# Two attention layers on one core: fewer, wider matmuls in the sums and the probability transposes, 256-wide visits, and the fetch of instructions in the builder's clock

## The chip, the cores and the metric

The kernel runs on one core of one Trainium2 chip. The metric is device time in microseconds (us). Two runs of the kernel before took 3495.84 and 3511.78 us, median 3503.81 us. A separate execution was recorded by the hardware profiler; every row in this document is from it.

## What is computed

The input x has 2048 rows of 512. Four layers follow each other, A, B, A, B, each on a layer-normalised x and added to x:

```
# A: 64 segments of 32 rows, one after the other; mem (8 rows) is handed on
for s in range(64):
    h = concat([mem, xs[s]])              # 40 x 512
    q, k, v = h @ Wq, h @ Wk, h @ Wv      # 32 heads of 128
    p = softmax(mask(q @ k.T * scale))    # 40 x 40 per head
    o = (p @ v) @ Wo
    mem = o[:8];  out[s] = o[8:]
# B: plain attention over all 2048 rows, 32 heads of 16, no mask
p = softmax(q @ k.T * 0.25);  out = (p @ v) @ wo
```

A is a recurrence: segment s+1 needs `mem` of segment s. B has no order of its own: a pair of a query block and a key block can be done as soon as both rows exist.

## The kernel before, in words

One Python program writes the instructions of all engines. For TensorE (PE) it fixes the order by hand: a planner (`step`, line 372) keeps a clock for PE, ScalarE (ACT) and VectorE (DVE), `Clock` (line 40), with a cost in us for every group of instructions, and emits whichever group its clock says is ready.

**A segment of A** is cut into groups that `segment` (line 698) takes from a list, PLAN or PLAN_PAIRS (lines 638 and 639). Q0 to Q3 and K0 to K3 (`qk_group`, line 525) project eight heads each: 32 matmuls of 128x128 weights with 40 columns, into one PSUM bank, which ACT or DVE then copies to `a_QT` or `a_KT`. S0 and S1 (`s_group`, line 562) make the scores of 16 heads each; ACT takes the exponential, and DVE masks, sums and scales it into `a_pn`. T0 and T1 (`pt_group`, line 589) transpose the probabilities with matmuls against the identity. V0 and V1 (line 552) project the values, P0 and P1 (or the pairs A and B; lines 608 and 619) multiply probabilities and values, and W0 to W3 (line 630) apply Wo. After W3, DVE writes the next segment's memory rows (line 743). A segment has 608 matmuls, each preceded by its weight load: 1216 rows on PE.

A matmul that needs only part of the 128x128 array is placed in a part of it by `tile_position`: in S and T of the kernel before, four matmuls stand side by side in column tiles of 32. The query of a head has 40 rows, so S needs two of these tiles for each head.

**Layer B in the gaps.** When a tile of 128 rows has come out of A, `tile_done` (line 867) projects it to B's q, k and v, stores them in device memory, and `visits` (line 839) adds the pairs of blocks that have become possible as runs; c is the group of 512 rows that the tile belongs to, r its place in it. A run is one query block (128 to 512 wide) of eight head pairs against a list of key tiles, cut into units of at most 512 columns. A unit (`emit_qk`, line 424) is 4 matmuls for each key tile, an exponential on ACT in two instructions (lines 437 and 440), and 4 matmuls of probabilities with values (`pv_mm`, line 443), which add up in one PSUM bank, `b_oacc`. At a run's end DVE adds `b_oacc` to what was stored of that block. `quota` (line 689) says how many units a segment should take in, at most 13. With five units or more the segment uses PLAN_PAIRS.

The second A starts when the first B has finished its first 512 rows, and the second B's last units run alone after the last segment.

## Time and profile before

| | us |
|---|---|
| median of two runs | 3503.81 |
| the two runs | 3495.84, 3511.78 |
| profiled execution, its own time | 3476.14 |
| its span, first to last instruction | 3474.4 |
| PE busy (matmuls) | 3066.5 |
| ACT busy | 2491.6 |
| DVE busy | 1555.3 |

The profiled execution was 27.7 us shorter than the median of the two runs. "PEld" is the loading of weights, which overlaps the matmuls. In a row of a group, "x" is the number of instructions, then come the busy time, the mean duration of one in ns, and the idle time of the engine just before them with what ended it. "issue" there means that the engine waited for nothing that the profile shows. The duration of a matmul includes its way through the array; matmuls follow each other more closely than that.

### The profile page before, as it was taken

The page shows a single profiled execution, that of the slowest core. Times are in us where ns is not written, and L with a number is a line of the kernel's source. Part 1 is how long each engine was busy: PE and PEld are TensorE (multiplying, and loading weights), DVE is VectorE, ACT ScalarE, POOL GpSimd, SP SyncE. Part 2 cuts the span into 40 slices and gives each one's busy share as a digit, 9 for nine tenths or more (in the row PEclk, how much of TensorE's full clock was granted, in tenths as well). Part 3 has the DMA queues.
Part 4 walks back from the last instruction along what each step waited for, and adds up shares of the span by engine and source line. Part 5 has one row for each costly group of instructions (what it writes and reads, how often), then busy time and mean ns, then how long its engine had stood idle before and what let it go on. Part 6 is the DMA issues. An engine that isn't in the chain of part 4 may idle for free. (4 is left out here: it accounts for less than half of the span.)

```text
span 3474.4 us, 218836 instructions
## 1 busy us (share of the span) xinstructions
PE 3066.5 (88%) x101019; PEld 2354.8 (68%) x101019; DVE 1555.3 (45%) x4220; ACT 2491.6 (72%) x3384; POOL 400.5 (12%) x677
## 2 busy tenths in 40 slices
PE   3888999899999889988889999989988899888998
PEld 2777777777676666656666767776666666666566
DVE  1223333355555445455445453435445455553411
ACT  1444667677778778867787676658777788887897
POOL 1000011111111111100111011111011111110000
PEclk9999999999999999989999999999999999999999
DMA  6000112232434335444343122324243343445431
GB/s 232 24 24 25 53 54 86 73 111 84 123 106 140 97 101 161 122 122 130 110 115 110 44 84 64 103 65 132 79 120 113 113 142 99 141 140 148 122 86 44
DMA packets 321695, 350.77 MB, mean 101 GB/s; under 512 B 95360, under 2 KB 248192, under 8 KB 320768
## 3 DMA queue, kind: packets, MB, share of 16 engines
q1 hardware_dynamic: 279792, 225.23, 23.2%
q0 software_dynamic: 35200, 102.55, 9.0%
q8 instruction: 791, 12.96, 1.6%
q10 hardware_dynamic: 5776, 8.91, 0.8%
q14 instruction: 136, 1.11, 0.1%
HBM read 234.02 MB, written 102.50 MB: 97 GB/s over the span
## 5 line engine op out<-in xcount | busy, mean ns | idle before, releaser
L437 ACT ACTIVATE b_pt<-b_SX 128x1536 bf16<-128x1536 f32 (+2 forms) x1040 | 1492.1, 1435 | 441.1 <-PE bank L435 401.5
L440 ACT ACTIVATE b_pt<-bank 128x512 bf16<-128x512 f32 (+2 forms) x1040 | 614.2, 591 | 1.4 <-PE bank L435 1.4
L533 PE MATMUL bank<-a_hT,a_Wq 128*128 128x40 bf16 x16384 | 504.1, 180 | 51.3 <-issue 20.7
L634 PE MATMUL bank<-a_OT,a_Wo 128*128 128x40 bf16 x16384 | 507.0, 183 | 47.8 <-ACT a_OT L249 24.1
L634 PEld LDWEIGHTS <-a_Wo 128*128 128x128 bf16 x16384 | 469.6, 98 | 97.4 <-issue 75.7
L533 PE MATMUL bank<-a_hT,a_Wk 128*128 128x40 bf16 x16384 | 504.4, 180 | 30.4 <-issue 21.6
L533 PEld LDWEIGHTS <-a_Wq 128*128 128x128 bf16 x16384 | 456.8, 96 | 102.0 <-issue 78.7
L533 PEld LDWEIGHTS <-a_Wk 128*128 128x128 bf16 x16384 | 456.5, 96 | 65.7 <-issue 54.8
L435 PE MATMUL b_SX<-b_q,b_k 32*128 32x128 bf16 (+2 forms) x6672 | 426.7, 271 | 46.2 <-ACT b_pt L437 18.1
L449 PE MATMUL b_oacc<-b_pt,b_v 128*17 128x128 bf16 (+2 forms) x8896 | 405.5, 272 | 28.4 <-issue 14.5
L435 PE MATMUL bank<-b_q,b_k 32*128 32x128 bf16 (+2 forms) x2224 | 414.9, 271 | 10.1 <-DVE a_KT L251 3.7
L251 DVE CAST a_OT<-bank 128x160 bf16<-128x160 f32 x689 | 194.8, 319 | 237.7 <-PE bank L604 231.7
L575 DVE TENSOR_TENSOR a_pn<-a_pn,c_mask 128x256 bf16<-128x256 bf16 x256 | 74.9, 293 | 498.0 <-ACT a_pn L573 497.6
L435 PEld LDWEIGHTS <-b_k 32*128 32x128 bf16 x8896 | 187.3, 94 | 160.2 <-issue 93.1
L548 PE MATMUL bank<-a_Wv,a_hT 128*32 128x512 bf16 x4096 | 272.6, 382 | 13.0 <-issue 7.9
L449 PEld LDWEIGHTS <-b_v 128*17 128x17 bf16 x8896 | 149.2, 90 | 175.7 <-issue 125.1
L813 DVE TENSOR_TENSOR b_ain<-b_oacc,b_ain 128x512 f32<-128x512 f32 (+2 forms) x248 | 165.5, 667 | 149.0 <-PE b_oacc L449 141.7
L818 POOL DMA_DIRECT2D b_A<-b_aout x200 | 108.7, 544 | 1066.7 <-DVE b_aout L806 902.2
L251 DVE CAST a_QT<-bank 128x320 bf16<-128x320 f32 x294 | 144.2, 490 | 187.1 <-PE bank L533 177.2
L818 POOL DMA_DIRECT2D b_A<-b_ain x176 | 95.7, 544 | 841.9 <-DVE b_ain L813 633.0
L251 DVE CAST a_KT<-bank 128x320 bf16<-128x320 f32 x259 | 126.8, 490 | 106.4 <-PE bank L533 89.8
L249 ACT CAST a_KT<-bank 128x320 bf16<-128x320 f32 x253 | 108.7, 430 | 91.2 <-PE bank L533 90.3
(111 smaller groups left out, 3484.9 us busy)
## 6 DMA issues: line engine op xcount, KB each, us to landing
b_ain<-b_A SPq DMA_DIRECT2D x224, 256.0 KB
b_A<-b_ain POOLq DMA_DIRECT2D x176, 256.0 KB, 3.1
b_k<-b_K SPq DMA_DIRECT2D x298, 128.0 KB
b_v<-b_V SPq DMA_DIRECT2D x456, 68.0 KB
b_q<-b_Q SPq DMA_DIRECT2D x240, 128.0 KB
b_A<-b_aout POOLq DMA_DIRECT2D x184, 64.0 KB, 2.6
a_rest<-a_vx POOLq DMA_DIRECT2D x64, 128.0 KB, 3.1
a_VR<-a_rest SPq DMA_DIRECT2D x512, 16.0 KB
```

The source lines that it names most:

```text
L249: self.nc.scalar.copy(dst, src)
L251: self.nc.vector.tensor_copy(dst, src)
L435: nc.tensor.matmul(out[t][:, j * qw:(j + 1) * qw], lhsT=k[32 * t:32 * t + 32, kj * 128:(kj + 1) * 128], rhs=q[32 * t:32 * t + 32, 0:qw], s ...
L437: nc.scalar.activation(pt[:, 0:NX, 0:w], self.SX[:, 0:NX, 0:w], ACT.Exp, scale=B_SCALE)
L440: nc.scalar.activation(pt[:, NX + i, 0:w], b.t[:, 0:w], ACT.Exp, scale=B_SCALE)
L449: self.nc.tensor.matmul(self.oacc[32 * t:32 * t + 17, 0:qw], lhsT=u.v[:, kj, 17 * t:17 * t + 17], rhs=u.p[:, t, j * qw:(j + 1) * qw], star ...
L533: nc.tensor.matmul(ps[:, u, :], lhsT=W[:, ft, h * DH:(h + 1) * DH], rhs=h_s[:, ft, 0:L], start=(n == 0) if ft_major else (ft == 0), stop=( ...
L548: self.nc.tensor.matmul(b.t[32 * t:32 * t + 32, :], lhsT=lhsT(ft), rhs=self.Wv[:, ft, n * 512:(n + 1) * 512], start=(ft == 0), stop=(ft == ...
L575: nc.vector.tensor_tensor(self.pn[:, st, :, M:L], self.pn[:, st, :, M:L], self.mask[:], ALU.mult)
L634: self.nc.tensor.matmul(ps[:, ft, :], lhsT=self.Wo[:, h, 128 * ft:128 * ft + 128], rhs=self.OT[:, h, :], start=(h == 0 and ft == 0), stop= ...
L813: nc.vector.tensor_tensor(acc[:, w], k.oacc[:, w], acc[:, w], ALU.add)
L818: nc.gpsimd.dma_start(B.Acc_d[self.qc][self.hg][:, self.qo:self.qo + self.qw], acc[:, w])
```

## The change

It has five parts.

1. **T**: one matmul transposes two heads. The identity's columns 0 to 39 and 64 to 103 are given as one operand of 80 columns (`sel`), so a T group has 16 matmuls of 80 columns where it had 32 of 40.
2. **S**: two column tiles of 64 in the place of four of 32, one matmul for each head: 16 matmuls where there were 32. `a_QT` gets 24 columns of padding behind every eight heads (`[128, 4, 8 * L + 24]`), because a tile of 64 reads 24 columns past the 40 of its head.
3. **B visits**: a query block of c > 0 that was taken as four runs of 128 columns is taken as two of 256, at r = 1 and r = 3. In the last group of 512 rows (c = 3) only r = 1 is 256 wide, and r = 2 and 3 stay at 128.
4. **The planner's clock** counts PE's instructions. At the 192nd of every 256 it notes the time, and the next 256 may not start before 3.7 us (`FETCH`) after that or after the fetch before. Each call of `pe` passes its number of matmuls, and some costs are changed by 0.02 to 0.1 us.
5. **The lists** PLAN and PLAN_PAIRS are in another order.

```
+FETCH = 3.7
 ...
     def pe(self, cost, ready, mode, n):
         t = max(self.t["PE"], ready) + (0.11 if mode != self.mode else 0.0)
         self.mode = mode
-        self.t["PE"] = t + cost
-        return t + cost + 0.18
+        left, per = 2 * n, cost / (2 * n)
+        while left:
+            step = min(left, (192 if self.count < 192 else 256) - self.count)
+            t, left, self.count = t + step * per, left - step, self.count + step
+            if self.count == 192:
+                self.ahead = t
+            elif self.count == 256:
+                t = max(t, self.fetched)
+                self.count, self.fetched = 0, max(self.fetched, self.ahead) + FETCH
+        self.t["PE"] = t
+        return t + 0.2
 ...
-        self.sel = [self.ident[:, 0:L], self.ident[:, 64:64 + L]]
+        self.sel = self.ident[:].rearrange("p (c r) -> p c r", c=2)[:, :, 0:L]
 ...
-        self.QT = bp.tile([128, H * L + 24], bf16, name="a_QT")
+        self.QT = bp.tile([128, 4, 8 * L + 24], bf16, name="a_QT")
 ...
+    def s_mm(self, ps, st, hp, ct):
+        h = 2 * (8 * st + hp) + ct
+        o = L * (h % 8)
+        self.nc.tensor.matmul(ps[64 * ct:64 * ct + 64, hp, :], lhsT=self.QT[:, h // 8, o:o + 64], rhs=self.KT[:, h, :], start=True, stop=True, tile_position=(0, 64 * ct))
 ...
         for hp in range(8):
-            for t in range(4):
-                h = 2 * (8 * st + hp) + t // 2
-                o = L * h + 32 * (t % 2)
-                nc.tensor.matmul(ps[32 * t:32 * t + 32, hp, :], lhsT=self.QT[:, o:o + 32], rhs=self.KT[:, h, :], start=True, stop=True, tile_position=(0, 32 * t))
-        done = ck.pe(0.29, max(at, self.s_at(st)), "PV")
+            for ct in range(2):
+                self.s_mm(ps, st, hp, ct)
+        done = ck.pe(0.27, max(at, self.s_at(st)), "col64", 16)
 ...
         for part in range(2):
-            for h4 in range(4):
+            for j in range(2):
                 for t in range(4):
-                    self.nc.tensor.matmul(ps[32 * t:32 * t + 32, 4 * part + h4, :], lhsT=self.pn[:, st, 2 * t + h4 // 2, 32 * part:32 * part + 32], rhs=self.sel[h4 % 2],
+                    self.nc.tensor.matmul(ps[32 * t:32 * t + 32, 4 * part + 2 * j:4 * part + 2 * j + 2, :], lhsT=self.pn[:, st, 2 * t + j, 32 * part:32 * part + 32], rhs=self.sel,
                                           start=True, stop=True, tile_position=(0, 32 * t))
 ...
-    PLAN = "Q0 K0 Q1 K1 S0 Q2 K2 Q3 K3 S1 T0 V0 P0 V1 T1 W0 P1 W1 W2 W3".split()
-    PLAN_PAIRS = "Q0 K0 Q1 K1 S0 Q2 K2 Q3 K3 S1 T0 V0 A0 B0 V1 T1 W0 A1 B1 W1 W2 W3".split()
+    PLAN = "K0 K1 Q0 Q1 Q2 S0 K2 Q3 K3 V0 S1 T1 T0 V1 P0 W0 P1 W1 W2 W3".split()
+    PLAN_PAIRS = "Q0 K1 K0 Q1 S0 Q3 K2 K3 Q2 S1 V1 T0 V0 B0 A0 T1 W0 A1 B1 W1 W2 W3".split()
 ...
-        if c > 0:
+        if c > 0 and (r == 1 or r == 3 and c < 3):
+            add(c, 128 * r - 128, 256, list(range(4 * c)))
+        elif c == 3 and r > 1:
             add(c, 128 * r, 128, list(range(4 * c)))
```

The planner then emits another order. Three places of it follow; what stands before and after is taken from the two built programs.

On PE, the start of the first T group of the program (`a_pn` holds the probabilities, `c_ident` is the identity). Before:

```order
L595 LDWEIGHTS a_pn
L595 MATMUL bank_222<-c_ident,a_pn 32x40
L595 LDWEIGHTS a_pn
L595 MATMUL bank_222<-c_ident,a_pn 32x40
L595 LDWEIGHTS a_pn
L595 MATMUL bank_222<-c_ident,a_pn 32x40
```

And of the change:

```order
L610 LDWEIGHTS a_pn
L610 MATMUL bank_220<-c_ident,a_pn 32x80
L610 LDWEIGHTS a_pn
L610 MATMUL bank_220<-c_ident,a_pn 32x80
L610 LDWEIGHTS a_pn
L610 MATMUL bank_220<-c_ident,a_pn 32x80
```

Each matmul writes 80 columns in the place of 40, and the group has 16 of them in the place of 32, each still with its own weight load.

On PE, the start of the first unit of the program whose query block is narrower than 512 (`b_SX` and a bank take the scores of the four row tiles). Before:

```order
L435 LDWEIGHTS b_k
L435 MATMUL b_SX<-b_q,b_k 128x128
L435 LDWEIGHTS b_k
L435 MATMUL b_SX<-b_q,b_k 128x128
L435 LDWEIGHTS b_k
L435 MATMUL b_SX<-b_q,b_k 128x128
L435 LDWEIGHTS b_k
L435 MATMUL bank_219<-b_q,b_k 128x128
```

And of the change:

```order
L447 LDWEIGHTS b_k
L447 MATMUL b_SX<-b_q,b_k 128x256
L447 LDWEIGHTS b_k
L447 MATMUL b_SX<-b_q,b_k 128x256
L447 LDWEIGHTS b_k
L447 MATMUL b_SX<-b_q,b_k 128x256
L447 LDWEIGHTS b_k
L447 MATMUL bank_222<-b_q,b_k 128x256
```

Such a unit has 8 score matmuls in the place of 16, and as many less with the values; its width on ACT, 512 columns, is the same.

On ACT, the third segment, which has no unit in it (`a_QT`, `a_KT`, `a_V` and `a_PT` are copies out of PSUM, the ACTIVATE is the exponential of S0 and of S1). Before:

```order
L249 CAST a_QT<-bank_220 128x320
L249 CAST a_KT<-bank_219 128x320
L249 CAST a_QT<-bank_222 128x320
L249 CAST a_KT<-bank_221 128x320
L249 CAST a_QT<-bank_220 128x320
L573 ACTIVATE a_pn<-bank_219 128x8x40
L249 CAST a_KT<-bank_222 128x320
L249 CAST a_QT<-bank_221 128x320
L249 CAST a_KT<-bank_220 128x320
L249 CAST a_PT<-bank_219 128x320
L249 CAST a_V<-bank_222 128x512
L573 ACTIVATE a_pn<-bank_221 128x8x40
```

And of the change:

```order
L261 CAST a_KT<-bank_219 128x320
L261 CAST a_KT<-bank_220 128x320
L261 CAST a_QT<-bank_222 128x320
L261 CAST a_QT<-bank_221 128x320
L261 CAST a_QT<-bank_219 128x320
L588 ACTIVATE a_pn<-bank_220 128x8x40
L261 CAST a_KT<-bank_222 128x320
L261 CAST a_QT<-bank_221 128x320
L261 CAST a_KT<-bank_219 128x320
L261 CAST a_V<-bank_220 128x512
L588 ACTIVATE a_pn<-bank_222 128x8x40
L261 CAST a_PT<-bank_221 128x320
```

The projections of K come first, the third Q group still stands ahead of S0, V0 comes ahead of S1, and T0 (`a_PT`) behind it.

Counted over both programs, PE's rows of the four layers, each matmul with its weight load (the kernel before has 2330 matmuls that only keep PE busy, the change 2509):

| rows on PE | before | change |
|---|---|---|
| S, 256 groups | 16384 | 8192 |
| T, 256 groups | 16384 | 8192 |
| units of B: scores and values | 35584 | 26368 |
| matmuls that keep PE busy | 4660 | 5018 |

And by stretch of the A layers, cut at the last Wo matmul of a segment (segments are counted from 0 over both A layers; units in equivalents of 512 columns):

| segments | rows before | rows of the change | units before | units of the change |
|---|---|---|---|---|
| 1 to 16 | 20096 | 18048 | 0 | 0 |
| 17 to 32 | 21376 | 18928 | 57 | 52 |
| 33 to 63 | 47296 | 40504 | 270 | 266 |
| 64 to 66 | 5832 | 5252 | 56 | 55 |
| 67 to 80 | 24284 | 21228 | 127 | 135 |
| 81 to 127 | 70972 | 60600 | 371 | 363 |
| behind the last | | | 143 | 153 |

Segments 53 to 55 have 5536 rows and 29 units before, and 4192 rows and 29 units in the change.

## Rows read from the trace of the kernel before

**Rows 1.** The page: span and busy time of each engine.

```profile
span 3474.4 us, 218836 instructions
PE 3066.5 (88%) x101019; PEld 2354.8 (68%) x101019; DVE 1555.3 (45%) x4220; ACT 2491.6 (72%) x3384; POOL 400.5 (12%) x677
```

**Rows 2.** The page: the chain that ended last, by engine.

```profile
PE 27%; issue 9%; ACT 9%; DVE 2%; DMA 1%; POOL 1%; SPq 0%; ACTq 0%; POOLq 0%; DVEq 0%
```

**Rows 3.** The page, DMA queues: packets, MB, share of 16 engines; PE's instructions.

```profile
q8 instruction: 791, 12.96, 1.6%
```

**Rows 4.** The same queue in the window 157 to 185 us.

```profile
q8 instruction: 8, 0.13, 1.8%
```

**Rows 5.** The same queue in the window 1081 to 1129 us.

```profile
q8 instruction: 12, 0.20, 1.8%
```

**Rows 6.** Timeline, PEld, 184 to 201 us: start, length, what, [idle before].

```profile
186.70 0.87 PEld L533 LDWEIGHTS <-a_Wq 128*128 128x128 bf16 x32
187.60 0.27 PEld L570 LDWEIGHTS <-a_QT 128*32 128x32 bf16 x31
...
195.06 0.85 PEld L634 LDWEIGHTS <-a_Wo 128*128 128x128 bf16 x31 [0.73 <-issue]
195.94 0.27 PEld L595 LDWEIGHTS <-a_pn 128*32 128x32 bf16 x32
196.25 0.87 PEld L634 LDWEIGHTS <-a_Wo 128*128 128x128 bf16 x32
197.15 0.10 PEld L604 LDWEIGHTS <-a_V 32*128 32x128 bf16 x4
...
197.32 0.10 PEld L604 LDWEIGHTS <-a_VR 8*128 8x128 bf16 x4
197.46 0.10 PEld L634 LDWEIGHTS <-a_Wo 128*128 128x128 bf16 x1
198.22 1.85 PEld L634 LDWEIGHTS <-a_Wo 128*128 128x128 bf16 x63 [0.66 <-issue]
```

**Rows 7.** Waits: engine and line, total us, times, longest us.

```profile
PEld L533 <- issue: 133.5, 320, 12.7
PEld L449 <- issue: 125.1, 429, 2.5
```

**Rows 8.** Busy time by stretch; window, length, PE PEld DVE ACT POOL, PEclk, DMA.

```profile
78.00:367.00 289.00, 252.72 (x10044) 217.54 (x10041) 89.62 (x260) 126.96 (x308) 21.69 (x32) 1.00 0.10 27
367.00:684.00 317.00, 291.42 (x10697) 234.86 (x10694) 122.05 (x336) 210.20 (x373) 34.13 (x55) 0.99 0.22 63
684.00:1451.00 767.00, 697.50 (x23658) 531.53 (x23655) 408.33 (x1081) 591.46 (x731) 106.31 (x183) 0.96 0.39 114
1451.00:1614.00 163.00, 138.72 (x2972) 90.55 (x2969) 85.28 (x248) 118.99 (x150) 15.18 (x26) 0.92 0.46 137
1614.00:1994.00 380.00, 337.27 (x12170) 264.11 (x12167) 186.91 (x515) 285.34 (x358) 40.47 (x67) 0.96 0.35 97
1994.00:3144.00 1150.00, 1032.05 (x35480) 790.87 (x35477) 567.87 (x1503) 867.92 (x1142) 151.81 (x259) 0.96 0.37 107
3144.00:3475.00 331.00, 293.15 (x5362) 207.49 (x5358) 83.49 (x240) 280.15 (x304) 19.87 (x35) 0.98 0.35 100
```

**Rows 9.** The same for segments 50 and 51, and 53 to 55.

```profile
1081.00:1129.00 48.00, 43.89 (x1392) 31.49 (x1390) 28.29 (x73) 43.07 (x51) 5.46 (x11) 1.00 0.56 166
1164.00:1246.00 82.00, 69.40 (x2779) 55.96 (x2772) 36.70 (x107) 60.72 (x70) 8.10 (x16) 0.96 0.28 76
```

**Rows 10.** Groups of instructions over the whole span.

```profile
L437 ACT ACTIVATE b_pt<-b_SX 128x1536 bf16<-128x1536 f32 (+2 forms) x1040 | 1492.1, 1435 | 441.1 <-PE bank L435 401.5 <-PE b_SX L435 14.4 <-PE bank L604 1.1
L440 ACT ACTIVATE b_pt<-bank 128x512 bf16<-128x512 f32 (+2 forms) x1040 | 614.2, 591 | 1.4 <-PE bank L435 1.4
L570 PEld LDWEIGHTS <-a_QT 128*32 128x32 bf16 x8192 | 99.6, 94 | 67.5 <-issue 23.6 <-ACT a_QT L249 11.6 <-DVE a_QT L251 9.7
```

More of the change, by code (lines that the diff above doesn't have):

```diff
@@ L45, in __init__, with pe @@
         self.mode = None
-    def pe(self, cost, ready, mode):
+        self.count, self.fetched, self.ahead = 0, 0.0, 0.0
+    def pe(self, cost, ready, mode, n):
         t = max(self.t["PE"], ready) + (0.11 if mode != self.mode else 0.0)
         self.mode = mode
-        self.t["PE"] = t + cost
-        return t + cost + 0.18
+        left, per = 2 * n, cost / (2 * n)
[9 more added lines that the diff above has]
+        return t + 0.2
     def cost(self, eng, n):
@@ L299, in transposes @@
             self.nc.tensor.transpose(ps[:, ft, :], xn[:, ft * 128:(ft + 1) * 128], self.ident[:])
-        done = self.ck.pe(0.25, max(ready, at), "full")
+        done = self.ck.pe(0.25, max(ready, at), "full", 4)
         dst(ps)
@@ L421, in keep_warm @@
             self.nc.tensor.matmul(b.t[:, 0:128], lhsT=self.ident[:], rhs=self.ident[:], start=True, stop=True)
-        b.free = ck.pe(0.056 * n, at, "full")
+        b.free = ck.pe(0.056 * n, at, "full", n)
     def emit_qk(self, u):
@@ L430, in emit_qk @@
         ys = [self.take() for _ in range(4 - NX)]
-        done = ck.pe(0.25, max([self.x_free, u.at, u.run.at] + [at for _, at in ys]), "S")
+        done = ck.pe(0.23, max([self.x_free, u.at, u.run.at] + [at for _, at in ys]), "S", 4 * len(u.kjs))
         out = [self.SX[:, i, :] for i in range(NX)] + [b.t[:] for b, _ in ys]
@@ L445, in pv_mm @@
         nj = len(u.kjs)
-        done = self.ck.pe(0.23, max(u.pt_at, self.o_free if u.first else 0.0), "PV")
+        done = self.ck.pe(0.23, max(u.pt_at, self.o_free if u.first else 0.0), "PV", 4 * nj)
         for j, kj in enumerate(u.kjs):
@@ L623, in pv_pair @@
         dst = self.pv_mms(st, ts, [b.t[:] for b, _ in bs])
-        done = self.ck.pe(0.26, max([ready] + [at for _, at in bs]), "S")
+        done = self.ck.pe(0.19, max([ready] + [at for _, at in bs]), "S", 16)
         w = 4 * L
@@ L665, in a_ready @@
         return max(t, self.bank_at())
-    MODE = {"Q": "full", "K": "full", "W": "full", "S": "PV", "T": "PV", "V": "PV", "P": "S", "A": "S", "B": "S"}
+    MODE = {"Q": "full", "K": "full", "W": "full", "S": "col64", "T": "PV", "V": "PV", "P": "S", "A": "S", "B": "S"}
     def a_pick(self, left):
@@ L878, in xo @@
                 nc.tensor.transpose(ps[:, ft, :], k.oTa[:, ft, :], k.ident[:])
-            done = ck.pe(0.25, max(at, k.at["oTa"]), "full")
+            done = ck.pe(0.25, max(at, k.at["oTa"]), "full", 4)
             xr = k.lnp.tile([128, 512], A.dt, name="a_xr", tag="xin", bufs=2)
@@ L898, in proj @@
                     nc.tensor.matmul(ps[:, g, :], lhsT=k.WB[:, ft, col + 128 * g:col + 128 * g + 128], rhs=k.hB[:, ft, :], start=(ft == 0), stop=(ft == 3))
-            return b, ps, ck.pe(0.95, at, "full")
+            return b, ps, ck.pe(0.95, at, "full", 16)
         c, r = divmod(Tt, 4)
@@ L919, in vv @@
                 nc.tensor.matmul(b.t[:], lhsT=k.hB[:, ft, :], rhs=k.WB[:, ft, 1024:1536], start=(ft == 0), stop=(ft == 3))
-            done = ck.pe(0.87, at, "full") + 0.2
+            done = ck.pe(0.87, at, "full", 4) + 0.2
             b.free = k.evac(k.vst[:, :, :, 0:16], b.t[:].rearrange("p (a b d) -> p b a d", b=2, d=16), 512, done, "DVE")
@@ L945, in tq @@
                 nc.tensor.transpose(ps[:, q, :], acc[:, 128 * q:128 * q + 128], k.identf[:])
-            done = ck.pe(0.09 * nq, at, "full")
+            done = ck.pe(0.11 * nq, at, "full", nq)
             v = ps[:, 0:nq].rearrange("p q (t s) -> p q t s", s=32)
@@ L982, in a @@
                 nc.tensor.transpose(ps[:, f, :], k.Osb[:, qs, f * 128:(f + 1) * 128], k.ident[:])
-            done = ck.pe(0.25, max(at, ready), "full")
+            done = ck.pe(0.25, max(at, ready), "full", 4)
             st["o"] = k.lnp.tile([128, 4, 128], bf16, name="b_OT", tag="t", bufs=3)
@@ L991, in b @@
                 nc.tensor.matmul(b.t[:], lhsT=st["o"][:, f, :], rhs=k.WoB[:, f, :], start=(f == 0), stop=(f == 3))
-            done = ck.pe(0.87, at, "full") + 0.2
+            done = ck.pe(0.87, at, "full", 4) + 0.2
             x = k.accp.tile([128, 512], self.out_dt, name="b_xo", tag="acc")
@@ L1024, in softmax @@
             for ct in range(2):
-                h = 2 * (8 * st + hp) + ct
-                nc.tensor.matmul(ps[64 * ct:64 * ct + 64, hp, :], lhsT=k.QT[:, L * h:L * h + 64], rhs=k.KT[:, h, :], start=True, stop=True, tile_position=(0, 64 * ct))
+                k.s_mm(ps, st, hp, ct)
         t = k.lnp.tile([128, 8, L], f32, name="g_t")
```

12 lines of the change are left out of this document (6 added, 6 removed).

## The prediction

> **What bounds the kernel now.** The page's busy shares come first [rows 1]: PE is busy for 88% of the span, ACT for 72%, and no other engine reaches half. A busy PE need not be at its limit, so the chain of waits comes next [rows 2]: PE 27% and ACT 9% of the span are on the chain with work, but 9%, some 310 us, is "issue", time in which PE waited for nothing that the profile shows. PE's instruction queue explains it [rows 3]: 791 packets of 12.96 MB are 16.4 KB each, and 791 x 256 = 202,496 is PE's number of rows (twice 101,019 by [rows 1]). So PE's program arrives in blocks of 256 rows. In a stretch without any unit of B, 8 blocks came in 28 us [rows 4]: 3.5 us a block, 13.7 ns a row. The timeline shows who waits [rows 6]: two "issue" gaps of 0.73 and 0.66 us at 195.06 and 198.22, and between them 31 + 32 + 32 + 32 (eight rows of four) + 1 = 128 loads, with their matmuls 256 rows, exactly a block. PE had finished one block and the next was not there. The largest sums of such waits are 133.5 and 125.1 us [rows 7]. At 3.5 us, 791 blocks are 2770 us, more than ACT's 2491.6.
>
> The limit is not the same everywhere. In segments 50 and 51, with 10 or 11 units each, 12 blocks came in 48 us [rows 5], 4.0 us a block, so the fetch had slack, and ACT was busy for 43.07 of 48 us [rows 9]: there ACT limits. In segments 53 to 55 with nearly as many units, but narrow ones, 5536 rows at 13.7 ns are 76 of 82 us and ACT is at 74% [rows 9]: there the fetch limits. The stretches [rows 8] give the mixture: ACT is busy for 44% in segments 1 to 16, 66% in 17 to 32, and 75 to 77% from 33 on (73% in 64 to 66, around the change of layers).
>
> **What the change removes.** By the tables of the order, S and T lose 8192 PE rows each, the units of B 9216, and 358 keep-warm rows are added: 25,242 fewer, 12%. No column less passes through PE: S had eight rounds of four matmuls of 40 columns and has eight rounds of two; T had eight rounds of 40 and has four of 80; a unit has half the matmuls, twice as wide. So what is saved is nearly all fetch, at 13.7 ns a row, and only where the fetch limits. By stretch, full value first, then the share that I take:
>
> - Segments 1 to 16: 2048 rows, 28 us. ACT is idle for more than half the time, so nearly all counts; the turn of the recurrence at each segment's end stays. 0.9: 25 us.
> - 17 to 32: 2448 rows, 33.5 us. ACT has room on the whole. 0.85: 28 us.
> - 33 to 63: 6792 rows, 93 us. The share is taken from segments 53 to 55: they lose 1344 rows, 18.4 us, so the fetch would allow 82 - 18 = 64 us; but their 29 units, at the 48 / 21 = 2.29 us a unit that segments 50 and 51 needed, want 66 us, and two limits so close do not overlap fully; I put them at 70, a saving of 12 of 18.4, or 0.65. Segments that ACT limits already give less; 0.6: 56 us.
> - 64 to 66: 580 rows, 8 us; the ends of the first B stand in it. 0.6: 5 us.
> - 67 to 80: 3056 rows, 42 us, but eight units more, each 1.435 + 0.591 = 2.03 us on ACT [rows 10]. 0.5: 21 us.
> - 81 to 127: 10,372 rows, 142 us, like 33 to 63. 0.6: 85 us.
>
> That is 220 us. **What it gives back:** 153 units in the place of 143 stand behind the last segment, where ACT is busy for 85% [rows 8]; ten at 2.03 us cost 20 us. The sum is 200 us less.
>
> **What I cost at nothing.** The padding of `a_QT`: S0 reads 24 columns that the third Q group writes, and its loads waited 11.6 + 9.7 us for those copies [rows 10]. The fetch goes on during such a wait, so these 21 us are mostly part of the fetch's time; between 0 and 21 us, I take 0. The wider tile of S: from the last projection load (its row of 32 loads ends at 187.57 with one of about 0.10 us, so it starts at 187.47) to the first load of S at 187.60 [rows 6] are 0.13 us, against 0.025 us between loads within a group: a change of tiling costs 0.10 us. S1 now stands with a tiling of its own among V and T, two changes more in each of 128 segments, 26 us of PE time. They fall where PE waits for blocks or for ACT; between 0 and 26 us, I take 0. "TensorEngine Tiling (Array Packing)" of the Trainium skill, under Key Properties, says that changing the tiling mode drains the engine, not just changing the tile. The gap in this row agrees; a sum that let every drain be felt would have 174 us for the gain. The fewer loads and stores of B and the fewer ends of runs on DVE: DMA is 1% of the chain and DVE 2% [rows 2], 0 us. The lists and the planner's clock move V0 ahead of S1 and T0 behind it, so that T0, V1, P0 and W0 lie beside S1's softmax; that and where units are placed could cost as well as gain. ACT's largest idle sum is 401.5 us of waits for the scores [rows 10]; I let a tenth of it, 40 us, go either way and take 0.
>
> **The number.** The profiled execution took 3476 us; less 200 is 3276. The median of the runs was 27.7 us higher than that execution, and the change should be measured like it: **3304 us**, 5.7% less. Unknown sizes: with every share at 1 the gain is 347 - 20 + 21 = 348 us, 3156 us; with 0.9 and 0.6 in the first two stretches, 0.3 from 33 on and 0 in 67 to 80, it is 25 + 20 + 28 + 2 + 43 - 20 = 98, less 26 for the tilings, 72 us, 3432 us. I expect neither end: the first needs ACT to limit nothing, the second sets segments 53 to 55 at half of what their rows allow. The forecast's own range is 3215 to 3425.
>
> **Rivals.**
>
> - *ACT takes over at once.* If every segment from 33 on behaves like 50 and 51, only the first 32 gain: 25 + 28 - 20 = 33 us, 3471 us. For it: ACT is at 90% there, and the number of units is the same. Against it: 53 to 55 have as many units and take 3.3 us a segment longer, with ACT at 74%. Chance 0.12.
> - *The blocks are not the limit.* If the gaps of PE come from elsewhere and a block always arrives in time, fewer rows save nothing and the ten late units cost 20 us: 3524 us. For it: the profile names no releaser of these gaps. Against it: 256 rows between two gaps and 3.5 us between blocks, whatever PE does in between. 0.07. The Trainium skill has this as its rule: "Runtime: NRT & Kernel Launch", Instruction fetch mechanics, says that the next block is fetched while the present one runs and that the cost of crossing a block is mostly hidden. By that rule the rival's time holds; the trace here disagrees, with 0.73 and 0.66 us lost at two crossings.
> - *The planner gains more.* With a clock that knows the fetch, ACT waits less for its scores: all shares near 0.9 and 40 of the 401.5 us are about 330 us, 3174 us. For it: the old clock knew no fetch and placed units by times that were too early. Against it: the order is only as good as its costs, and 3.7 us stands where the trace has 3.5. 0.08.
> - *Slower: the clock of PE.* PE's granted clock is 1.00 in segments 1 to 16, but 0.92 in 64 to 66, 1 being 2.4 GHz and a half 1.2 GHz [rows 8]. With the same work in fewer rows and ACT limiting more, PE may stand still more often and fall to the lower level; a microsecond there costs up to half a microsecond. To lose the 200 us and 70 more, PE needs 540 us more at 1.2 GHz, a mean clock about 0.08 lower than now: 3574 us. It decides from there. Against it: in segments 1 to 16 PE has no matmul running for 13% of the time, and the clock stays at 1.00. 0.04.
>
> **Chances.** The forecast has 0.69. A measurement of this kernel can tell about 2% from no change, that is 70 us: faster is below 3434. The range that holds 8 of 10 takes in the forecast, most of the planner's case and the part of ACT's case nearest to the forecast: 3185 to 3440. Faster: 0.69 + 0.08 + a quarter of ACT's case, 0.80. Same: the rest of it and the hidden fetch, 0.16. Slower: 0.04.
>
> **What would show it.** PE's instruction queue should have about (202,038 - 25,242) / 256 = 691 packets. In segments 1 to 16 the spacing of blocks should stay near 3.5 us, and a segment without units take 15.4 in the place of 17 us. In segments 53 to 55 ACT should rise to about 85% and the time fall to 70 us. The waits of S's loads for `a_QT` should be gone. The stretch behind the last segment should be some 20 us longer. I am wrong if the blocks become rarer and the segments are not shorter, if ACT's idle time before the scores grows by as much as the fetch gives, or if the granted clock falls below 0.9.

## The result and the profile after

The kernel after the change takes **3344.9 us** (median of two runs, 3343.7 and 3346.1) against 3503.8 before, a ratio of 0.955 with a 95% interval of 0.945 to 0.964. Predicted were 3304 us. In the sets of runs below, the kernel before was run 29 more times: medians of 3517.6, 3516.1 and 3516.8 us in three sets, single runs from 3501 to 3530. The changed kernel, run again beside them, took 3345.5, a ratio of 0.953 (0.949 to 0.957). So the change is worth about 171 us, of which 159 showed against the two runs of before that the prediction had.

**A caution about the rows of before.** The profiled execution of before (span 3474.4) is shorter than all of those 29 runs. A comparison by stretch with [rows 8] alone is therefore some 40 us too small in sum. One experiment (`p6_act_load`, below) runs the instructions of before unchanged from segment 17 on and gives a second profile of them; the table below uses both.

**The page.** Span, engines, and PE's instruction queue (packets, MB, share), to be set beside [rows 1] and [rows 3]:

```profile
span 3344.4 us, 192793 instructions
PE 3058.7 (91%) x88348; PEld 2263.6 (68%) x88398; DVE 1526.7 (46%) x4077; ACT 2495.4 (75%) x3439; POOL 357.7 (11%) x597
...
q8 instruction: 693, 11.35, 1.4%
```

98 blocks of 256 rows fewer, 693 in the place of 791; 691 were predicted. PE is busy for 3058.7 us, before for 3066.5: what went is almost all time in which PE stood idle (286 us of the span, 408 before).

Busy time by stretch, after, as in [rows 8]: window, length, PE PEld DVE ACT POOL, PEclk, DMA. The windows end at the last Wo matmul of segments 16, 32, 63, 66, 80 and 127:

```profile
78.00:350.50 272.50, 247.60 (x9020) 212.36 (x9023) 90.83 (x263) 122.70 (x304) 21.68 (x32) 0.99 0.11 28
350.00:653.00 303.00, 285.15 (x9478) 226.19 (x9479) 126.34 (x337) 195.60 (x356) 30.86 (x49) 0.98 0.21 61
653.00:1386.00 733.00, 693.14 (x20257) 502.19 (x20259) 387.25 (x1006) 595.39 (x763) 90.43 (x154) 0.95 0.37 108
1386.00:1545.00 159.00, 135.94 (x2644) 84.75 (x2648) 84.86 (x243) 113.61 (x144) 17.18 (x30) 0.90 0.48 138
1545.00:1915.00 370.00, 338.98 (x10638) 254.76 (x10641) 188.98 (x515) 298.89 (x374) 35.66 (x59) 0.96 0.34 94
1915.00:3005.00 1090.00, 1023.17 (x30297) 748.36 (x30308) 553.01 (x1435) 858.89 (x1155) 131.44 (x221) 0.95 0.35 102
3005.00:3345.00 340.00, 311.04 (x5449) 217.77 (x5453) 83.64 (x239) 299.74 (x324) 19.36 (x34) 0.99 0.35 96
```

Every stretch up to segment 127 is shorter, the one behind it is longer, and ACT's share rises where B is dense (33 to 63: from 77% to 81%). The column PEclk says that the granted clock did not rise: 0.95 and 0.95 in the two long stretches, against 0.96 and 0.96.

In us, each stretch by the two profiles of either kernel (before: the profile shown ahead and `p6_act_load`; after: its profile and that of `after_again`), and the last column for `u4_old_lists`, the changed kernel with before's lists of group order:

| segments | before | after | gain, of the means | predicted | gain of `u4_old_lists` |
|---|---|---|---|---|---|
| 1 to 16 | 289.3 | 272.9, 270.7 | 17.5 | 25 | 18.1 |
| 17 to 32 | 316.9, 326.7 | 302.7, 300.6 | 20.1 | 28 | 19.2 |
| 33 to 63 | 767.0, 771.9 | 732.6, 733.5 | 36.4 | 56 | 49.9 |
| 64 to 66 | 162.6, 162.6 | 159.6, 161.1 | 2.3 | 5 | 2.8 |
| 67 to 80 | 379.8, 389.6 | 370.1, 369.2 | 15.0 | 21 | 16.0 |
| 81 to 127 | 1150.6, 1158.3 | 1090.0, 1092.0 | 63.5 | 85 | 78.8 |
| behind 127 | 330.0, 329.3 | 338.9, 339.5 | -9.6 | -20 | -27.6 |

The sum of the gains is 145 us; some 26 of the 171 of the medians lie in the difference between these two profiles of before and its usual run. For segments 1 to 16 there is a second profile of before's instructions too, `p3_visits_256` below, which has the same ones there and took 301.4 us at a granted clock of 0.95 (289.3 at 1.00). The gain of 17.5 us is the one at a like clock.

Groups of the page after, which answer to the first two of [rows 10] (busy, mean ns | idle before, releaser):

```profile
L449 ACT ACTIVATE b_pt<-b_SX 128x1536 bf16<-128x1536 f32 (+1 forms) x1040 | 1493.7, 1436 | 337.0 <-PE bank L447 296.2
L452 ACT ACTIVATE b_pt<-bank 128x512 bf16<-128x512 f32 (+1 forms) x1040 | 616.2, 593 | 1.4 <-PE bank L447 1.2
```

ACT does the same 1040 exps and waits 296.2 us for the scores, 105 less than before. The weight loads of S (L577) and T (L610) after, from the groups of PEld:

```profile
L577 PEld LDWEIGHTS <-a_QT 128*64 128x64 bf16 x4096 | 85.3, 112 | 70.8 <-issue 54.1 <-DVE a_V L263 7.3 <-DVE a_QT L263 2.5
L610 PEld LDWEIGHTS <-a_pn 128*32 128x32 bf16 x4096 | 53.4, 98 | 61.0 <-DVE a_pn L598 45.2 <-issue 5.6 <-DVE c_okm L281 0.4
```

S's loads wait 2.5 us for DVE's copy of `a_QT` where they waited 9.7, and 1.9 us (outside the three releasers shown) for ACT's, where they waited 11.6 [rows 10]: the waits that should be gone are 4.4 us of 21.3, and none with before's lists of group order. The loads' waits without a releaser ("issue") have gone up, from 23.6 to 54.1. That is not PE waiting longer for S's instructions, since a load can also stand idle while its matmul waits for data (as at Wo, below): such waits at the matmuls of S fell from 16.7 to 0.9 us.

### The profile page after: what moved, and what is told of

Its sections match the earlier page's. It is cut to its first block, busy times and chain, and to the rows that moved or that the text cites. A ratio compares the mean times of both kernels' runs of the same rounds, so it can differ in the third digit from the quotient of the medians.

```text
span 3344.4 us, 192793 instructions
## 1 busy us (share of the span) xinstructions
PE 3058.7 (91%) x88348; PEld 2263.6 (68%) x88398; DVE 1526.7 (46%) x4077; ACT 2495.4 (75%) x3439; POOL 357.7 (11%) x597
## 4 chain that ended last, share of the span: by engine, by line
PE 61%; ACT 17%; issue 14%; DVE 4%; DMA 3%; POOL 1%; SPq 0%; ACTq 0%; POOLq 0%; DVEq 0%
PE bank L545 21%; PE bank L649 12%; ACT b_pt L449 12%; PE b_SX L447 8%; PE bank L560 6%; PE b_oacc L461 4%; ACT b_pt L452 2%; PE bank L619 2%; PE bank L915 2%; PE bank L577 1%; ACT a_pn L588 1%; PE bank L447 1%; PE bank L936 1%; ACT a_V L261 1%; PE bank L610 1%
## 5 line engine op out<-in xcount | busy, mean ns | idle before, releaser
L449 ACT ACTIVATE b_pt<-b_SX 128x1536 bf16<-128x1536 f32 (+1 forms) x1040 | 1493.7, 1436 | 337.0 <-PE bank L447 296.2
L452 ACT ACTIVATE b_pt<-bank 128x512 bf16<-128x512 f32 (+1 forms) x1040 | 616.2, 593 | 1.4 <-PE bank L447 1.2
L545 PE MATMUL bank<-a_hT,a_Wq 128*128 128x40 bf16 x16384 | 480.3, 180 | 34.1 <-ACT a_KT L261 17.5
L545 PEld LDWEIGHTS <-a_Wq 128*128 128x128 bf16 x16384 | 443.3, 96 | 78.8 <-issue 68.5
L447 PE MATMUL b_SX<-b_q,b_k 32*128 32x512 bf16 (+3 forms) x4944 | 424.0, 309 | 49.4 <-ACT b_pt L449 32.8
L447 PE MATMUL bank<-b_q,b_k 32*128 32x512 bf16 (+3 forms) x1648 | 411.5, 309 | 9.7 <-DVE b_xo L1011 4.2
L461 PE MATMUL b_oacc<-b_pt,b_v 128*17 128x512 bf16 (+3 forms) x6592 | 398.8, 306 | 6.8 <-DVE b_ain L828 3.6
L447 PEld LDWEIGHTS <-b_k 32*128 32x128 bf16 x6592 | 157.5, 92 | 168.5 <-issue 107.7
L461 PEld LDWEIGHTS <-b_v 128*17 128x17 bf16 x6592 | 123.3, 89 | 167.2 <-issue 133.7
L619 PE MATMUL bank<-a_PT,a_V 32*128 32x40 bf16 x2896 | 162.3, 182 | 37.1 <-ACT a_V L261 16.5
L619 PEld LDWEIGHTS <-a_V 32*128 32x128 bf16 x4096 | 117.8, 93 | 105.2 <-issue 39.9
L433 PE MATMUL bank<-c_ident 128*128 128x128 bf16 x2509 | 172.3, 221 | 0.1
```

Source lines behind the costliest of these rows:

```text
L433: self.nc.tensor.matmul(b.t[:, 0:128], lhsT=self.ident[:], rhs=self.ident[:], start=True, stop=True)
L447: nc.tensor.matmul(out[t][:, j * qw:(j + 1) * qw], lhsT=k[32 * t:32 * t + 32, kj * 128:(kj + 1) * 128], rhs=q[32 * t:32 * t + 32, 0:qw], s ...
L449: nc.scalar.activation(pt[:, 0:NX, 0:w], self.SX[:, 0:NX, 0:w], ACT.Exp, scale=B_SCALE)
L452: nc.scalar.activation(pt[:, NX + i, 0:w], b.t[:, 0:w], ACT.Exp, scale=B_SCALE)
L461: self.nc.tensor.matmul(self.oacc[32 * t:32 * t + 17, 0:qw], lhsT=u.v[:, kj, 17 * t:17 * t + 17], rhs=u.p[:, t, j * qw:(j + 1) * qw], star ...
L545: nc.tensor.matmul(ps[:, u, :], lhsT=W[:, ft, h * DH:(h + 1) * DH], rhs=h_s[:, ft, 0:L], start=(n == 0) if ft_major else (ft == 0), stop=( ...
```

## The experiments

Four theories. **Theory 1**: PE is held by the arrival of its instructions, so the number of rows decides. **Theory 2**: PE's own work decides. **Theory 3**: the builder's new clock and lists make the gain. **Theory 4**: through the change ScalarE has become what sets the pace in B. The runs were made in three sets of four, each beside its own runs of before.

| run | rows against before | median us | before | ratio (95%) |
|---|---|---|---|---|
| `p1_t_wide` | -8192 | 3449.7 | 3517.6 | 0.981 (0.977 to 0.984) |
| `p2_s_two_tiles` | -8192 | 3435.3 | 3517.6 | 0.977 (0.974 to 0.980) |
| `p3_visits_256` | about -8700 | 3413.8 | 3517.6 | 0.971 (0.968 to 0.974) |
| `p4_clock_lists` | about -300 | 3520.2 | 3517.6 | 1.001 (0.999 to 1.003) |
| `u1_s_four_tiles` | about -17,000 | 3396.7 | 3516.1 | 0.965 (0.962 to 0.968) |
| `u2_t_narrow` | about -17,000 | 3381.0 | 3516.1 | 0.961 (0.959 to 0.963) |
| `u3_no_fetch_in_clock` | about -25,200 | 3359.1 | 3516.1 | 0.955 (0.953 to 0.957) |
| `u4_old_lists` | about -24,900 | 3332.6 | 3516.1 | 0.948 (0.945 to 0.950) |
| `after_again` | about -25,200 | 3345.5 | 3516.8 | 0.953 (0.949 to 0.957) |
| `u5_old_visits` | about -16,700 | 3403.5 | 3516.8 | 0.969 (0.966 to 0.971) |
| `u6_act_load` | about -25,200 | 3381.2 | 3516.8 | 0.961 (0.958 to 0.964) |
| `p6_act_load` | 0 | 3548.4 | 3516.8 | 1.010 (1.007 to 1.013) |

**One part of the change alone, on the kernel before.** The transposes:

```
-            for h4 in range(4):
-                ... matmul(ps[32*t:32*t+32, 4*part + h4, :], ..., rhs=self.sel[h4 % 2], ...)
+            for j in range(2):
+                ... matmul(ps[32*t:32*t+32, 4*part + 2*j:4*part + 2*j + 2, :], ..., rhs=self.sel, ...)
```

> The kernel before, with one probability transpose per head pair and nothing else of the change; the order of groups on every engine stays. 4096 pairs of load and matmul fewer, 8192 instruction rows, 32 blocks of 256 rows. Theory 1 (TensorE is held by the arrival of its instructions): 8192 x 13.7 ns is 112 us if every row were waited for; the whole change gave 159 of the 351 us that its rows would have been worth, a share of 0.45, so about -50 us here, 3454 (3410 to 3490). Theory 2 (only TensorE's own work counts): the group of transposes takes 0.19 instead of 0.27 us, 256 groups, -20 us, 3484. Theory 3 (the gain comes from the builder's new order): nothing, 3504.

The sums:

```
-            for t in range(4):
-                ... matmul(ps[32*t:32*t+32, hp, :], lhsT=self.QT[:, o:o + 32], rhs=self.KT[:, h, :], ...)
+            for ct in range(2):
+                self.s_mm(ps, st, hp, ct)     # 64 columns of the padded QT
```

> The kernel before, with the sums in two column tiles of 64 and the padded Q transposes that these need; no planner cost is changed, so the order stays. 8192 rows fewer, as many as in the run of the transposes alone. Theory 1 (arrival of instructions): the same as there, about -50 us, 3454 (3410 to 3490). Theory 2 (TensorE's own work): the sums' group takes 0.33 instead of 0.27 us in the trace of the kernel after, 256 groups, +15 us, 3519. Theory 3 (new order): nothing, 3504. This run and the one of the transposes drop equally many rows but change TensorE's own work with opposite signs.

The visits:

```
-        if c > 0:
+        if c > 0 and (r == 1 or r == 3 and c < 3):
+            add(c, 128 * r - 128, 256, list(range(4 * c)))
+        elif c == 3 and r > 1:
```

> The kernel before, with visits of 256 columns to B and nothing else. 9216 rows fewer, all of them in segments 33 to 127, where ScalarE is busy over 80%. Theory 1 (arrival of instructions): worth 126 us in full; with the share of 0.37 to 0.43 that these stretches showed about -50 us, 3454 (3400 to 3490). Theory 2 (TensorE's own work): the same columns are moved, some -10 us at most, 3494. Theory 3 (order): the visits are the planner's work, so a new order comes with them; a gain of any size up to -100 could be from it.

The clock, the lists and the padding, with every instruction of the layers of before (170 matmuls that only keep PE busy are fewer):

```
+FETCH = 3.7
...
+    def pe(self, cost, ready, mode, n):      # with the count of blocks
...
+    PLAN = "K0 K1 Q0 Q1 Q2 S0 K2 Q3 K3 V0 S1 T1 T0 V1 P0 W0 P1 W1 W2 W3".split()
```

> The kernel before, with the builder's clock that counts blocks of instructions, the new lists of group order and the padded Q transposes, and all the instructions of before: sums in four tiles, transposes per head, visits of 128 columns. No row is dropped. Theory 1 (arrival of instructions): the number of blocks is what counts, so within 25 us of 3504. Theory 3 (the new order makes the gain): most of the 159 us, 3400 or less. Rival to both: the new order was sought for the new instructions and costs something with the old ones, 3520 to 3560.

Measured: -68, -82 and -104 us for the three that drop rows, and +3 for the one that drops next to none, within its interval of no change. That is theory 1. The three gave more than its middle value, 8.3, 10.0 and 12.0 ns for each row dropped (13.7 would be the full value). Theory 2 falls with the first two: it wanted -20 and +15. Its premise was wrong as well: all loads of S together are 85.3 us after the change against 99.6 before [rows 10], not more. PE's busy time with the matmuls of T fell from 106.5 to 86.7 us, and with those of S from 123.3 to 113.3; so some 20 of the 68 us and 10 of the 82 may be PE's own work, not more. The sums came out 14 us better than the transposes with as many rows, but the intervals overlap (-56 to -81 and -72 to -93 us), so that difference is not settled. The visits are the least clean of the three: they also place the units anew, read less from device memory (211 MB against 234) and have fewer ends of runs on DVE, and no run separates these from their rows. Theory 3 falls with the fourth, as far as the clock and the lists go.

That the fourth shows nothing in sum hides two movements. Its segments 33 to 63, 81 to 127, and the stretch behind 127 (as in [rows 8]):

```profile
692.50:1463.20 770.70, 705.80 (x23634) 531.32 (x23633) 411.82 (x1086) 591.83 (x729) 105.94 (x182) 0.94 0.40 115
2023.80:3204.60 1180.80, 1060.04 (x35820) 805.88 (x35824) 568.25 (x1499) 887.64 (x1169) 153.69 (x262) 0.94 0.38 106
3204.60:3514.70 310.10, 275.52 (x4880) 192.73 (x4876) 82.33 (x237) 260.94 (x284) 18.28 (x32) 0.97 0.36 102
```

The stretch behind the last segment is 20 us shorter than before, segments 81 to 127 are 22 to 30 longer, and PE's granted clock is 0.94 in both long stretches against 0.96 [rows 8].

**One part taken back, on the kernel after.** The sums in four tiles again, with the padding kept:

```
-            for ct in range(2):
-                self.s_mm(ps, st, hp, ct)
+            for t in range(4):
+                ... matmul(ps[32*t:32*t+32, hp, :], lhsT=self.QT[:, h // 8, o:o + 32], ...)
```

> The changed kernel, with the sums back in four column tiles; the padding, the planner's costs and the order stay. 8192 rows come back, 32 blocks. Theory 1 (arrival of instructions): 0.4 to 0.45 of 112 us, +45 to +50, 3392. Theory 2 (TensorE's own work): the group of sums is shorter by 0.06 us, 256 groups, -15 us, 3330. Theory 3 (order): nothing, 3345.

The transposes per head again:

```
-            for j in range(2):
+            for h4 in range(4):
```

> The changed kernel, with one transpose per head again; the order stays. 8192 rows come back. Theory 1 (arrival of instructions): +45 to +50 us, 3392. Theory 2 (TensorE's own work): the group takes 0.08 us more, 256 groups, +20 us, 3365. Theory 3 (order): nothing, 3345.

The builder's clock without the blocks:

```
-        left, per = 2 * n, cost / (2 * n)
-        while left:
-            ...
+        self.t["PE"] = t + cost
+        return t + cost + 0.2
```

> The changed kernel, with the fetch taken out of the builder's clock: the same instructions, planned as if none were ever late. Theory 1 (arrival of instructions): the number of blocks is unchanged, so what changes is only which work stands in which hole: within 30 us of 3345. Theory 3 (the new order makes the gain): most of the 159 us is lost, 3450 and over.

The lists of before:

```
-    PLAN = "K0 K1 Q0 Q1 Q2 S0 K2 Q3 K3 V0 S1 T1 T0 V1 P0 W0 P1 W1 W2 W3".split()
+    PLAN = "Q0 K0 Q1 K1 S0 Q2 K2 Q3 K3 S1 T0 V0 P0 V1 T1 W0 P1 W1 W2 W3".split()
```

(and `PLAN_PAIRS` in the same way)

> The changed kernel, with the two lists of group order of the kernel before; the same instructions in another order inside each segment. Theory 1 (arrival of instructions): within 30 us of 3345. Theory 3 (the new order makes the gain): most of the 159 us is lost, 3450 and over.

Measured against the 3345 of the changed kernel: +52 for the sums, +36 for the transposes, +14 for the clock, -12 for the lists. Theory 1 holds for the sums and is 10 us too high for the transposes; theory 2's -15 for the sums is excluded. Theory 3 is excluded by both of its runs. As the last step each part is worth less than as the first: 52 of 82, 36 of 68; a later run adds the visits, 58 of 104.

With the old lists the kernel is the fastest of all, and its rows show why it isn't faster still. The same three stretches:

```profile
651.70:1371.30 719.60, 678.91 (x20226) 496.43 (x20224) 385.39 (x1006) 587.92 (x754) 89.74 (x152) 0.97 0.38 109
1899.80:2975.50 1075.70, 1004.97 (x30178) 741.69 (x30180) 548.98 (x1427) 844.54 (x1147) 130.40 (x219) 0.98 0.35 102
2975.50:3332.80 357.30, 327.38 (x5713) 228.41 (x5712) 84.04 (x240) 315.01 (x340) 19.91 (x35) 0.99 0.34 94
```

13 and 14 us shorter in the two long stretches than after, at a granted clock of 0.97 and 0.98, and 18 us longer behind the last segment, where ACT has 340 instructions in the place of 324. So the new lists bring units forward out of the last stretch and pay for it in the segments, as in the kernel with all the old instructions.

**The control, the visits, and ScalarE.** The changed kernel as it is, with no edit:

> The changed kernel as it is, beside the others of this set on the same chip. From its own runs 3345 of 3516, a ratio of 0.951 (0.948 to 0.955). With the old lists of group order it was 3333 in an earlier set, a ratio of 0.9475 (0.945 to 0.950): if the order of the new lists costs time, the ratio here lies above 0.950; if the two are the same, inside that interval.

Its ratio, 0.953, is above that of the old lists, 0.948, but the intervals touch (0.949 and 0.950). So the version with the old lists is faster than the changed kernel by some 12 us as far as one can tell, and clearly faster than the one before, by 5.2%.

Visits of 128 columns again:

```
-        if c > 0 and (r == 1 or r == 3 and c < 3):
-            add(c, 128 * r - 128, 256, list(range(4 * c)))
-        elif c == 3 and r > 1:
+        if c > 0:
```

> The changed kernel, with the visits of 128 columns to B again, 9216 rows more, all from segment 33 on. Theory 1 (arrival of instructions, and less of it the more has been taken away): alone the visits gave 104 us; the sums gave 82 alone and 52 as the last step, the transposes 68 and 36, so some 0.58 of 104, +60 us, 3405. Theory 4 (ScalarE now sets the pace from segment 33 on, so that rows there cost little): +25 us or less, 3370.

Measured: +58 us, theory 1's 60 and not theory 4's 25. Rows that stand in B's visits are still paid for where ACT is busiest. Segments 33 to 63 and 81 to 127 of this kernel:

```profile
655.30:1417.60 762.30, 706.57 (x21648) 524.36 (x21642) 409.52 (x1084) 593.57 (x730) 105.79 (x182) 0.94 0.40 115
...
1951.20:3082.00 1130.80, 1047.75 (x32718) 784.47 (x32720) 566.85 (x1501) 880.07 (x1161) 152.96 (x261) 0.95 0.39 110
```

Without the wide visits, segments 33 to 63 take 762 us, little less than before (767 and 772), though S and T have their fewer rows; the clock there, 0.94, is part of that. The visits alone brought the same stretch to 726 us:

```profile
693.80:1419.50 725.70, 669.95 (x22210) 503.96 (x22208) 390.71 (x1018) 586.46 (x741) 89.73 (x152) 0.99 0.38 109
```

The old lists with all three edits have 719.6 there (above), at a granted clock of 0.97 where the visits alone had 0.99: with the visits made, the fewer rows of S and T add 6 us in these segments. On the kernel before they gave more, 759.0 us with the transposes alone and 751.5 with the sums alone, 10 and 18 us below the mean of before.

S and T stand alone in segments 1 to 16, where B has nothing: before 289.3 [rows 8], the transposes alone (first row) 282.2, the sums alone 283.0, both (with the new lists and the old visits) 270.8.

```profile
77.90:360.10 282.20, 249.53 (x9536) 213.23 (x9536) 89.59 (x260) 126.22 (x308) 21.71 (x32) 1.00 0.10 28
```

```profile
77.80:360.80 283.00, 253.81 (x9538) 216.50 (x9536) 89.55 (x260) 124.93 (x308) 21.68 (x32) 0.99 0.10 28
```

```profile
77.30:348.10 270.80, 246.30 (x9025) 211.24 (x9024) 90.91 (x264) 122.65 (x304) 21.68 (x32) 1.00 0.10 28
```

512 matmuls fewer are worth 14 us at 13.7 ns a row; the first step gave half of that, the second nearly all, at the same clock. Why the first gives only half isn't settled, and one profile each is little to go by. The visits alone change nothing in these segments, and still took 301.4 us, 12 more than before, at a lower granted clock:

```profile
77.50:378.90 301.40, 260.00 (x10048) 224.40 (x10048) 89.56 (x260) 126.86 (x308) 21.67 (x32) 0.95 0.10 26
```

More work for ScalarE, on the kernel after and on the one before:

```
+        self.nx += 1
+        if self.nx % 2:
+            nc.scalar.copy(self.xload[:], self.ident[:, 0:64])
```

> The changed kernel, with one more copy of 128x64 on ScalarE after every second exp, 520 copies of about 0.22 us, 115 us of ScalarE work that nobody waits for; the order stays. Theory 4 (after the change ScalarE sets the pace in B's visits from segment 33 on): three quarters of it shows, +85 us, 3430 or more. Theory 1 alone (arrival of instructions still sets the pace, ScalarE has slack): a third, +40 us, 3385.

> The kernel before, with the same 520 copies on ScalarE. Theory 4 (ScalarE has taken over through the change): less than in the changed kernel, +45 us, 3562, since 0.16 to 0.19 of ScalarE's time was free here from segment 33 on against 0.11 to 0.14 there. If the same amount shows in both kernels, ScalarE's part in the pace has not changed and the smaller yield of the later edits has another cause.

Measured: +36 and +32 us. **This pair did not test theory 4.** The copies depend on nothing, and they did not stay behind their exps. In the changed kernel (ns min/median/max, first and last start):

```profile
L457 ACT COPY c_xload<-c_ident x520: 242/244/277, 40.9 to 240.8; 128x64 bf16<-128x64 bf16 x174
```

All 520 ran within the first 241 us, before B is dense. They made segments 1 to 16 longer by some 30 us, nearly all of what they cost, at a granted clock that fell to 0.92:

```profile
81.40:382.80 301.40, 257.80 (x9026) 221.72 (x9024) 90.55 (x264) 211.12 (x755) 21.68 (x32) 0.92 0.10 26
```

(The expectation also put ScalarE's free share too low: by [rows 8] and the rows after, it is 0.23 to 0.25 before from segment 33 on and 0.19 to 0.21 after.) The segments from 17 on are those of the kernels without the copies, and that makes the second run useful as a second profile of the instructions of before (segments 17 to 32, 33 to 63, 67 to 80 and 81 to 127):

```profile
403.10:729.80 326.70, 291.73 (x10692) 234.05 (x10695) 122.18 (x336) 211.38 (x373) 34.13 (x55) 0.99 0.22 61
729.80:1501.70 771.90, 694.62 (x23650) 528.02 (x23649) 408.79 (x1082) 592.17 (x731) 106.29 (x183) 0.97 0.40 113
1664.30:2053.90 389.60, 340.20 (x12168) 266.19 (x12167) 186.71 (x514) 285.52 (x358) 40.48 (x67) 0.95 0.35 95
2053.90:3212.20 1158.30, 1034.54 (x35496) 793.87 (x35500) 567.90 (x1503) 869.14 (x1143) 151.84 (x259) 0.96 0.38 106
```

At nearly the same clock they are 0.6 to 3.1% longer than [rows 8]: that is how far one profile's stretch can be trusted.

## Why the prediction was right, and where its sizes were off

**The limit: right.** Dropping 8192 rows gave 68 us in one place and 82 in another, while an altered plan with all rows gave none. The rival "the blocks are not the limit" is out, and with it the rule by which it went: the Trainium skill, "Runtime: NRT & Kernel Launch", Instruction fetch mechanics, has the cost of crossing a block mostly hidden; here the edits save 8 to 12 ns for each row dropped.

PE's own waits show it directly. Before, PE stood still 215 times for over 0.15 us with no releaser in the profile, 131 us in all (156 in the second profile); after, 67 times, 27 us (28 in the second profile). The row of the projections before and the one after (total us, times, longest):

```profile
PE bank L533 <- issue: 42.3, 68, 1.8
```

```profile
PE bank L545 <- issue: 16.3, 35, 1.5
```

Before, 214 of the 215 end 1.1 to 1.7 us after a packet of PE's instruction queue has landed, in the median 1.4; of PE's waits with a named releaser 13% do. If PE's sequencer merely handed on rows at a fixed pace, or the data were late, the waits would not keep that distance from the packets. They come back with the rows: 66 us with the sums in four tiles, 44 with the narrow transposes, 63 with the old visits. They are not the whole loss, since shorter waits are not counted: in segments 1 to 16 they were 10.7 us, and the gain is 17.5.

**One piece of evidence for it: misread.** The two gaps of 0.73 and 0.66 us [rows 6] are not late blocks. Both stand at loads of Wo, and the loads stand behind matmuls whose releaser the profile names (timeline of PE, before):

```profile
195.06 0.96 PE L634 MATMUL bank<-a_OT,a_Wo 128*128 128x40 bf16 x32 [0.75 <-ACT a_OT L249]
...
198.22 0.95 PE L634 MATMUL bank<-a_OT,a_Wo 128*128 128x40 bf16 x24 [0.68 <-ACT a_OT L249]
```

Such waits in segments 1 to 16, before:

```profile
PE bank L634 <- ACT a_OT L249: 16.6, 24, 0.8
```

and after (total us, times, longest):

```profile
PE bank L649 <- ACT a_OT L261: 17.0, 24, 0.8
```

The matmuls of Wo wait for ACT's copy of `a_OT`, before as after; that 256 rows lay between two such waits was a coincidence. So luck had a part: the conclusion was right, this support for it was not. The sums of [rows 7] are of loads and mix both kinds of wait; PE's own were 131 us. Late blocks look otherwise: most cut a group in the middle, where no new data is waited for. After, in the third group of projections (start, length, what, [idle before]):

```profile
182.13 0.48 PE L545 MATMUL bank<-a_hT,a_Wq 128*128 128x40 bf16 x13
183.18 0.40 PE L545 MATMUL bank<-a_hT,a_Wq 128*128 128x40 bf16 x9 [0.57 <-issue]
```

The price of a block [rows 4] did not hang on the two gaps, so the sum stood.

**The shares: mis-sized.** This is the term of the sum that was off. No part alone reached the full 13.7 ns a row, and the shares of it were too high. Measured by the table above, they are 0.63 of 28 us where 0.9 was taken (1 to 16), 0.60 of 33.5 for 0.85, 0.39 of 93 for 0.6, 0.29 of 8 for 0.6, 0.36 of 42 for 0.5, and 0.45 of 142 for 0.6.

In 33 to 63 and 81 to 127 the traces show why, segment by segment. In 33 of these 78 segments ACT was busy for 80% or more before (mean of the two profiles). They lost rows worth 62 us at 13.7 ns, with 332 units before and after, and came out 2 us longer. The other 45 lost rows worth 174 us and came out 102 us shorter, a share of 0.59; with before's lists it is 10 of 62 and 118 of 178. So the prediction's two kinds of segment were right. For the second kind its 0.65 was near; where ACT was that busy, fewer rows gave nothing or next to it, and the 0.6 for all of them together hardly allowed for that. Segments 50 and 51, its example of ACT's limit, took 47.8 us before and 47.7 after.

A second reason is that the worth of a row falls as rows go: the parts alone gave 68 + 82 + 104 = 254 us, the whole gives 171 (184 with before's lists), and each part as the last step gave less than as the first. The prediction priced the whole by one share for each stretch and had no such term. The blocks fit this: of the 790 intervals between them before, 420 were shorter than 3.9 us, near the pace at which blocks can come (354 in the second profile); of the 692 after, 223 (247).

In segments 1 to 16 ACT has room, and the reason is not shown. PE's wait for `a_OT` stays at 17 us there, but it is no longer than before and so doesn't explain a smaller gain by itself.

**Segments 53 to 55: right.** 70 us with ACT at 85% were predicted. After:

```profile
1114.50:1185.70 71.20, 66.59 (x2097) 49.86 (x2097) 33.99 (x95) 60.67 (x73) 3.89 (x8) 0.93 0.20 56
```

71.2 us, and ACT is busy for 60.67 of them, 85%. But the gain here is that of the visits, with 960 of the 1344 rows: alone they bring these segments from 81.8 us to 67.0 (at a granted clock of 1.00, before 0.96; after the whole change it was 0.93), the sums alone to 78.7 and the transposes alone to 81.2. These were the segments with the narrowest units, and the share of 0.65 that they gave was carried over to all of 33 to 63 and 81 to 127, where S and T, over half of the rows, bring less than the units do.

**The spacing of blocks and the pure segment: missed, by the same term.** In segments 1 to 16, 70 blocks came in 272.5 us, 3.9 us a block where about 3.5 was predicted and 78 in 289 had been 3.7. An ordinary segment there, without units, takes 16 us in the median, not 15.4 (17 before).

**What it gives back: half as much.** The stretch behind the last segment is 9.6 us longer, not 20. The ten units are there and cost ACT the 20 us that were predicted (busy for 280 us before, 300 after). But ACT had 51 us without work in that stretch before and has 40 after; half of the new work went into that time. The prediction took ACT's work for time. This error, 10 us the other way, hides a part of the first one in the sum. With before's lists 18 more units than before stand there, and the stretch is 27.6 us longer.

**Costed at nothing.** The padding's wait fell from 21 us to 4.4. No run isolates the padding or the changes of tiling; the sums alone, which bring both, gave 82 of at most 112 us, so they can't have cost more than 30 together, if a row is worth 13.7 ns at most. The clock and the lists were to lie within 40 us: +3 as one part on the kernel before; in the kernel after the lists cost some 12 and the clock saves some 14, neither quite clear of its interval. In the single stretches this is not nothing, and it is part of the miss: with the old lists, segments 33 to 63 gain 49.9 and 81 to 127 gain 78.8 us, close to the 56 and 85 predicted.

**The rivals.** "ACT takes over at once" is wrong for the rows of visits (58 us for taking them back), and half right for those of S and T in segments 33 to 63. By segment it is right for the 33 in which ACT was busy for 80% or more, and wrong for the others. No run with more ACT work in B was made, so how much room ACT has left there stays open. "The clock of PE" named an effect that hardly shows: over its six runs the changed kernel has a mean granted clock of 0.949 to 0.960, the kernel before in its 29 runs of 0.953 to 0.969, not the 0.08 less that would have decided.

## What to carry to other kernels

Where an engine is busy for 90% with small instructions, count its instruction blocks by stretch and divide: if they come at a pace that doesn't change when the work does, the number of instructions is the cost, and merging matmuls that share a shape pays even if PE's columns stay the same. Take the share of that gain by segment: where another engine was busy for 80% or more, fewer rows gave nothing here. Price each such edit as the last one too, since the second and third find less left to save; and take a wait for a late block from gaps in the middle of a group, not from gaps at its start, where data may be late. Change the order of work and the instructions in separate runs: here the instructions made all of the gain, and the new order cost some of it.
